# Half-and-half head layout for the first seven attention tiles, a key ring, and a new place for one gating product

## The chip, the cores and the metric

One Trainium2 chip, one of its cores. The metric is the device time of one execution in microseconds (us), taken over several runs; a trace of one profiled execution stands beside them. The engines are TensorE (PE in the rows; PEld is its weight load), VectorE (DVE), ScalarE (ACT), GpSimd (POOL) and SyncE (SP), which issues the transfers. A "q" behind an engine's name (DVEq) marks what its sequencer does.

## The reference

Local attention with a few global keys and a distance bias, followed by a channel mix with a sigmoid gate, all in float32. Cut to what matters:

```python
# q, k, v: (4, 8, 768, 64); n_global = 8; n_local = 96
scores = q @ k.T / 8 + bias(distance, head)      # kept where key < n_global or 0 <= rel < n_local
a = softmax(where(keep, scores, -1e9))
x = (a @ v) as (4, 768, 512)
xk, xr = mu * x + (1 - mu) * x_prev              # x_prev: one position earlier
out = sigmoid(xr @ w_r) * (relu(xk @ w_k) ** 2 @ w_v)
```

w_k is 512x1024, w_v 1024x512, w_r 512x512.

## The kernel before

The 3072 query rows are 24 tiles of 128 rows, six to a batch entry; t is a tile's place in its entry. The channel mix works on 12 chunks of two tiles each.

Attention, per tile (functions `load_tile`, `split_tile`, `scores`, `transposes`, `weighted`): queries and keys come with the 64 head dimensions on partitions. A tile's scores use 256 key columns, the 128 of the tile before (whose first 32 are replaced by the entry's first 32 keys from t = 2 on, because the global keys lie there) and its own 128; at t = 0 there are only its own. Scores of two heads go into one PSUM tile `s`. VectorE adds the pattern and reduces (line 294), ScalarE takes exponentials (295), VectorE makes the reciprocal of the sums (301, 302), GpSimd scales (305), TensorE transposes (316), ScalarE copies the result out (317), and TensorE multiplies with the values (333).

The first seven tiles (`NATIVE = 7`, tiles 0 to 6) use plain float32 matmuls (line 286); all later ones use two float32r products of a high and a low part (288, 289). The first seven have their heads on the lower 64 partitions; the upper 64 of two query buffers `qz` and two key buffers `kz` are set to zero once by GpSimd (lines 204 and 205). Line 222 loads a tile's queries, 225 its keys; 227 loads the whole tile before at t = 1; 229 and 230 load the first 32 keys and the other 96 of the tile before from t = 2 on. All go to the buffer `n % 2`.

The weights come as 64-bit words and are turned into float32 by ScalarE or GpSimd and VectorE (159 to 172, `weight_begin`); `weight_split` then makes a high part (179) and a low part on VectorE (180). There are 20 pieces: eight of w_k, four of w_r, eight of w_v. Chunk 0 uses the words themselves (lines 385, 406 and 439), and the splits are given out one at a time beside it; the later chunks use high and low parts (376 to 378).

`channel_mix` makes four tiles kp (two blocks of 128 features each), two tiles z for the gate and two tiles vps; the gating product `sig = vps * sigmoid(z)` (446) is on VectorE, and 447 writes the result. kp, z and vps share three PSUM buffers in turn, so the second kp tile of chunk 1 needs the buffer of chunk 0's first vps tile, and the third one that of the second.

At the end stands a branch: if the sizes were outside what the patterns cover, a general version (`wide`) would run; with these inputs it is skipped. Seven small VectorE instructions (lines 621 to 627) make the flag from the sizes, every engine reads it (629), and line 630 branches.

The order of instructions on each engine is not the order of the text: when the kernel is built, a scheduler plays the program through a cost model and puts each engine's instructions into a queue, which the engine then works off in order. `tc.issue_after(ins)` adds edges to it: what the block holds is queued behind `ins` on that instruction's engine, without a semaphore.

Of the kernel before, what the change touches and what calls it, by code (L numbers as in the profile page):

```python
# [9 lines left out]
F32 = mybir.dt.float32  # L10
# [5 lines left out]
ALU = mybir.AluOpType  # L16
# [3 lines left out]
B, H, S, D = 4, 8, 768, 64  # L20
DM, DF = 512, 1024
NT = S // 128
NTILES = B * NT
NCHUNK = NTILES // 2
NATIVE = 7
GMAX = 32
LMAX = 97
# [5 lines left out]
def tile_biased_attention_channel_mix(ctx: ExitStack, tc: tile.TileContext, qT, kT, v, n_sizes, mu_kr, w_k, w_v, w_r, q_rows, k_rows, v_rows, slopes, out):  # L33
    nc = tc.nc
    vec, act, pool, pe = nc.vector, nc.scalar, nc.gpsimd, nc.tensor
# [8 lines left out]
    ngf, nlf = sizes[:, 0:1], sizes[:, 1:2]  # L44
# [22 lines left out]
    p4k = fast.enter_context(tc.tile_pool(name="p4k", bufs=3))  # L67
    kw_pool = fast.enter_context(tc.tile_pool(name="kw", bufs=2))
# [105 lines left out]
    def weight_split(i):  # L174

        name, src, k, c = w_steps[i]
        word, hi = w_word.pop((name, k, c)), w_hi[name][:, k, c : c + 512]
        lo = w_low[name, k, c] = w_pool.tile([128, 512], F32R, tag="wl", name=f"w{name}_lo_{i}")
        (act.copy if i % 4 < 2 else pool_copy)(hi, word)
        vec.tensor_sub(lo, word, hi)  # L180

    w_count = [0, 0]

    def weights_go(begun):
        while w_count[0] < min(begun, len(w_steps)):
            weight_begin(w_count[0])
            w_count[0] += 1

    def splits_go(n):
        while w_count[1] < n:  # L190
            weight_split(w_count[1])
            w_count[1] += 1

    def pool_copy(dst, src):
        pool.tensor_scalar(dst, src, 1.0, 1.0, op0=ALU.mult, op1=ALU.mult)


    state = {}

    padded = []  # L200
    for i in range(2):
        qz = q_pool.tile([128, H, 128], F32, name=f"qz_{i}", tag="qh")
        kz = kw_pool.tile([128, H, 256], F32, name=f"kz_{i}", tag="kw")
        pool.memset(qz[64:128], 0.0)
        pool.memset(kz[64:128], 0.0)
        padded.append((qz, kz))

    def load_tile(n):
        b, t = divmod(n, NT)
        s = state[n] = {}  # L210
        native = n < NATIVE
        halves = (0,) if native else (0, 64)
        if native:
            qr, kr = padded[n % 2]
        else:
            qr = p4k.tile([128, H, 128], F32, tag="t4k", name=f"qraw_{n}")
            if n == NATIVE:
                kr = kw_pool.tile([128, H, 256], F32, tag="kw", name=f"kraw_{n}")
            else:
                kr = p4k.tile([128, H, 128], F32, tag="t4k", name=f"kraw_{n}")  # L220
        for o in halves:
            nc.sync.dma_start(qr[o : o + 64], qT[n])
        for o in halves:
            if n <= NATIVE:
                nc.sync.dma_start(kr[o : o + 64, :, 128:256], kT[n])
                if t == 1:
                    nc.sync.dma_start(kr[o : o + 64, :, 0:128], kT[n - 1])
                elif t:
                    nc.sync.dma_start(kr[o : o + 64, :, 0:32], kT[n - t, :, :, 0:32])
                    nc.sync.dma_start(kr[o : o + 64, :, 32:128], kT[n - 1, :, :, 32:128])  # L230
            else:
                nc.sync.dma_start(kr[o : o + 64], kT[n])
        s["qr"], s["kr"] = qr, kr
# [13 lines left out]
    def split_tile(n):  # L247
        t = n % NT
        s = state[n]
        s["sum"] = s_pool.tile([128, H], F32, name=f"sum_{n}", tag="sum")  # L250
        s["nmax"] = s_pool.tile([128, H], F32, name=f"nmax_{n}", tag="nmax")
        s["e"] = {}
        if n < NATIVE:
            return
        qh = q_pool.tile([128, H, 128], F32R, name=f"qh_{n}", tag="qh")
        ql = q_pool.tile([128, H, 128], F32R, name=f"ql_{n}", tag="ql")
        kw = kw_pool.tile([128, H, 256], F32R, name=f"kw_{n}", tag="kw")
        cur = kw[:, :, 0 if n == NATIVE and t else 128 : 256]
        kr = s["kr"]
        if n == NATIVE:  # L260
            kr = kr[:, :, 256 - cur.shape[2] : 256]
        pool_copy(qh, s["qr"])
        pool_copy(cur, kr)
        vec.tensor_sub(ql, s["qr"], qh)
        vec.tensor_sub(cur[64:128], kr[64:128], cur[64:128])
        if t and n > NATIVE:
            pk = state[n - 1]["kw"]
            if t == 1:
                pool_copy(kw[:, :, 0:128], pk[:, :, 128:256])
            else:  # L270
                pool_copy(kw[:, :, 32:128], pk[:, :, 160:256])
                pool_copy(kw[:, :, 0:32], pk[:, :, 0:32])
        s["qh"], s["ql"], s["kw"] = qh, ql, kw

    def scores(n, hp):
        t = n % NT
        s = state[n]
        c0 = 0 if t else 128
        w = 256 - c0
        p = pat if t else pat0  # L280
        ps = ps_s.tile([128, 512], F32, name=f"s_{n}_{hp}", tag="s")
        for u in range(2):
            h = 2 * hp + u
            o = ps[:, u * 256 : u * 256 + w]
            if n < NATIVE:
                pe.matmul(o, s["qr"][:, h, :], s["kr"][:, h, c0:256], start=True, stop=True)
            else:
                pe.matmul(o, s["qh"][:, h, :], s["kw"][:, h, c0:256], start=True, stop=False)  # L288
                pe.matmul(o, s["ql"][:, h, :], s["kw"][:, h, c0:256], start=False, stop=True)  # L289
        for u in range(2):  # L290
            h = 2 * hp + u
            o = ps[:, u * 256 : u * 256 + w]
            e = e_pool.tile([128, 256], F32, name=f"e_{n}_{h}", tag="e")
            vec.tensor_tensor_reduce(out=e[:, :w], in0=o, in1=p[:, h, :], op0=ALU.add, op1=ALU.min, scale=-0.125, scalar=3.0e38, accum_out=s["nmax"][:, h : h + 1])  # L294
            act.activation(e[:, :w], e[:, :w], AF.Exp, bias=s["nmax"][:, h : h + 1], scale=-1.0, accum_out=s["sum"][:, h : h + 1])  # L295
            s["e"][h] = e
        if hp % 2 == 0:
            return
        h0, nh = 2 * hp - 2, 4
        r = s_pool.tile([128, nh], F32, name=f"r_{n}_{hp}", tag="r", bufs=8)  # L300
        vec.tensor_scalar(r, s["sum"][:, h0 : h0 + nh], 1.0e-9, None, op0=ALU.add)
        vec.reciprocal(r, r)  # L302
        for u in range(nh):
            e = s["e"][h0 + u]
            pool.tensor_scalar(e[:, :w], e[:, :w], r[:, u : u + 1], 1.0, op0=ALU.mult, op1=ALU.mult)  # L305
# [62 lines left out]
    def channel_mix(xk, xr, out_rows, f_pool, f2_pool, ps_f, first=False):  # L368
# [6 lines left out]
        def three(o, sh, sl, mh, ml, first, last):  # L375
            pe.matmul(o, sh, mh, start=first, stop=False)  # L376
            pe.matmul(o, sh, ml, start=False, stop=False)  # L377
            pe.matmul(o, sl, mh, start=False, stop=last)  # L378
# [14 lines left out]
        for fp in range(4):  # L393
# [5 lines left out]
            for u in range(2):  # L399
                f = slice((2 * fp + u) * 128, (2 * fp + u + 1) * 128)  # L400
                c = fp // 2 * 512
                g = slice(f.start - c, f.stop - c)
                o = ps[:, u * 256 : (u + 1) * 256]
# [28 lines left out]
        for i in range(2):  # L432
            c = slice(i * 128, (i + 1) * 128)
            vp = ps_f.tile([128, 512], F32, name="vps", tag="f")
            sig = sigs[i][1]
            for f in range(8):
                if first:
                    weights_go(13 + f)
                    pe.matmul(vp, kk_all[:, f, c], w_word["v", f, 0], start=f == 0, stop=f == 7)
                    if i:  # L440
                        splits_ok[0] = 13 + f
                else:
                    splits_go(13 + f)
                    three(vp, kkh[:, f, c], kkl[:, f, c], w_hi["v"][:, f, :], w_low["v", f, 0], f == 0, f == 7)
                yield
            vec.tensor_mul(sig, vp, sig)  # L446
            nc.sync.dma_start(out_rows(i), sig)

    splits_ok = [0]

    def ffn(c):
        xt = state["x", c]
# [25 lines left out]
    for step in range(NTILES + 1):  # L478
# [4 lines left out]
        for hp in range(4):  # L483
# [18 lines left out]
            n = min(8, 2 + slot * 4 // 3) if slot < 6 else 8 + (slot - 5) * 6 // 7  # L502
# [115 lines left out]

    okf = const.tile([128, 2], F32, name="okf")
    wide_i = const.tile([1, 1], I32, name="wide_i")  # L620
    vec.tensor_scalar(okf[:, 0:1], nlf, float(LMAX), None, op0=ALU.is_le)
    vec.tensor_scalar(okf[:, 1:2], nlf, 1.0, None, op0=ALU.is_ge)
    vec.tensor_mul(okf[:, 0:1], okf[:, 0:1], okf[:, 1:2])
    vec.tensor_scalar(okf[:, 1:2], ngf, float(GMAX), None, op0=ALU.is_le)
    vec.tensor_mul(okf[:, 0:1], okf[:, 0:1], okf[:, 1:2])
    vec.tensor_scalar(okf[:, 0:1], okf[:, 0:1], -1.0, 1.0, op0=ALU.mult, op1=ALU.add)
    vec.tensor_copy(wide_i, okf[0:1, 0:1])

    need_wide = nc.values_load(wide_i[0:1, 0:1], min_val=0, max_val=1)
    with tc.If(need_wide > 0):  # L630
# [45 lines left out]
```

## Time and profile before

| | before |
|---|---|
| time, median of 3 runs | 522.92 us (522.72 to 523.63) |
| the profiled execution | 522.1 us |
| its span, first to last instruction | 520.3 us |
| mean granted TensorE clock | 0.988 |
| TensorE busy | 499.3 us (96%) |
| VectorE busy | 359.4 us (69%) |
| HBM read, written | 41.16 MB, 6.29 MB |

The span is what the trace shows; the time has 1.8 us more around it. Busy times are those of one execution. TensorE's matmuls overlap, and their ends are modelled, so that a busy TensorE is not one at its peak. A granted clock of 1.00 is 2.4 GHz, 0.50 is 1.2 GHz.

### The profile page before, as it was taken

To read this page: it belongs to the slowest core of one execution; us is meant where nothing else is said; L and a number is where in the kernel's file an instruction comes from. 1 tells how busy PE (TensorE), PEld (TensorE's weight loads), DVE (VectorE), ACT (ScalarE), POOL (GpSimd) and SP (SyncE) were. 2 spreads that over 40 slices of the span, in tenths; PEclk is the share of its full clock that TensorE was granted. 3 is DMA by queue.
4 is the path that set the end of the run, shared out by engine and by line. 5 is a ranking of instruction groups with operands and counts; after the bars stand their busy time and mean duration, and the time that the engine had idled before them with its cause. 6 is when DMAs were issued, how large, how long until landed. Compare 5 with 4: busy or idle time off the path is not lost.

```text
span 520.3 us, 9815 instructions
## 1 busy us (share of the span) xinstructions
PE 499.3 (96%) x3420; PEld 427.1 (82%) x3420; DVE 359.4 (69%) x856; ACT 311.1 (60%) x712; POOL 253.7 (49%) x392
## 2 busy tenths in 40 slices
PE   7978999889999999999999999999999999999995
PEld 5656864488898898898898898898898898898984
DVE  6869989877878858757768858757768855435321
ACT  4869653244658567567668567567668568544220
POOL 7657847318658536427538536427538535203000
PEclk9979999989999999999999999999999999999999
DMA  8997952411432422422322522423322210100101
GB/s 196 326 247 174 233 197 66 122 41 42 111 93 66 127 63 67 108 81 83 103 62 66 126 64 67 109 80 82 101 62 67 71 38 25 42 7 2 40 2 45
DMA packets 27304, 48.16 MB, mean 93 GB/s; under 512 B 7216, under 2 KB 13360, under 8 KB 27248
## 3 DMA queue, kind: packets, MB, share of 16 engines
q1 hardware_dynamic: 27104, 47.46, 34.3%
q8 instruction: 29, 0.48, 0.4%
q14 instruction: 27, 0.22, 0.1%
q10 hardware_dynamic: 144, 0.00, 0.0%
HBM read 41.16 MB, written 6.29 MB: 91 GB/s over the span
## 4 chain that ended last, share of the span: by engine, by line
PE 79%; DVE 2%; DMA 1%; issue 0%; POOL 0%; SPq 0%; DVEq 0%; POOLq 0%
PE kp L376 8%; PE vps L377 8%; PE vps L376 8%; PE kp L377 8%; PE kp L378 8%; PE vps L378 8%; PE av L333 7%; PE t L316 6%; PE z L376 4%; PE z L377 4%; PE z L378 4%; PE s L289 3%; PE s L288 3%; DMA qraw<-in_qT_dram 1%; DVE wv_lo L180 1%
## 5 line engine op out<-in xcount | busy, mean ns | idle before, releaser
L305 POOL TENSOR_SCALAR e<-e,r 128x256 f32<-128x256 f32 (+1 forms) x192 | 104.2, 562 | 151.1 <-DVE r L302 88.4
L295 ACT ACTIVATE e<-e,nmax 128x256 f32<-128x256 f32 (+1 forms) x192 | 92.9, 485 | 27.9 <-DVE nmax L294 23.9
L376 PE MATMUL kp<-xk_hi,wk_hi 128*128 128x256 f32 x352 | 100.2, 285 | 4.2 <-DVE sig L446 4.2
L378 PE MATMUL kp<-xk_hi,wk_lo 128*128 128x256 f32 x352 | 99.5, 283 | 0.0
L377 PE MATMUL kp<-xk_lo,wk_hi 128*128 128x256 f32 x352 | 99.4, 282 | 0.0
L294 DVE CUSTOM_DVE_ANT_0 e<-s,pat 128x256 f32<-128x256 f32 (+1 forms) x192 | 69.1, 395 | 34.4 <-PE s L289 22.0
L376 PEld LDWEIGHTS kp<-xk_hi,wk_hi 128*128 128x128 f32 x352 | 67.0, 190 | 5.1 <-DVE sig L446 4.4
L377 PE MATMUL vps<-wv_lo,kk_hi 128*128 128x512 f32 x176 | 69.9, 397 | 0.0
L376 PE MATMUL vps<-wv_hi,kk_hi 128*128 128x512 f32 x176 | 69.9, 397 | 0.0
L378 PE MATMUL vps<-wv_hi,kk_lo 128*128 128x512 f32 x176 | 69.2, 393 | 0.0
L377 PEld LDWEIGHTS kp<-xk_lo,wk_hi 128*128 128x128 f32 x352 | 66.7, 190 | 0.4
L378 PEld LDWEIGHTS kp<-xk_hi,wk_lo 128*128 128x128 f32 x352 | 66.7, 190 | 0.0
L317 ACT COPY et<-t 128x512 f32<-128x512 f32 (+1 forms) x96 | 52.1, 545 | 17.1 <-PE t L316 16.6
L316 PE MATMUL t<-ident,e 128*128 128x128 f32 x352 | 57.2, 281 | 4.6 <-POOL e L305 4.2
L419 DVE TENSOR_TENSOR kk<-kp,kk 128x512 f32<-128x512 f32 x44 | 30.4, 690 | 43.9 <-ACT kk L413 43.7
L316 PEld LDWEIGHTS t<-ident,e 128*128 128x128 f32 x352 | 42.2, 142 | 17.8 <-POOL e L305 7.0
L333 PE MATMUL av<-et,va 128*64 128x128 f32 x704 | 46.6, 278 | 1.5 <-ACT et L317 1.5
L333 PEld LDWEIGHTS av<-et,va 128*64 128x64 f32 x704 | 39.0, 136 | 10.3 <-issue 5.7
L421 DVE TENSOR_TENSOR kk_lo<-kk,kk_hi 128x512 fp32r<-128x512 f32 x44 | 32.6, 742 | 17.3 <-ACT kk_hi L420 17.1
L413 ACT ACTIVATE kk<-kp 128x512 f32<-128x512 f32 x48 | 28.3, 590 | 23.8 <-PE kp L378 23.0
L420 ACT CAST kk_hi<-kk 128x512 fp32r<-128x512 f32 x44 | 27.3, 621 | 24.9 <-DVE kk L419 24.9
L288 PE MATMUL s<-kw,qh 128*128 128x256 f32 (+1 forms) x136 | 40.4, 320 | 0.0
(109 smaller groups left out, 1030.0 us busy)
## 6 DMA issues: line engine op xcount, KB each, us to landing
kraw<-in_kT_dram SPq DMA_DIRECT2D x36, 256.0 KB, 4.1
qraw<-in_qT_dram SPq DMA_DIRECT2D x34, 256.0 KB, 4.3
va<-in_v_dram SPq DMA_DIRECT2D x24, 256.0 KB, 3.1
out_dram<-sig SPq DMA_DIRECT2D x24, 256.0 KB, 3.5
w<-in_w_k_dram SPq DMA_DIRECT2D x8, 512.0 KB, 8.2
w<-in_w_v_dram SPq DMA_DIRECT2D x8, 512.0 KB, 3.6
kz<-in_kT_dram SPq DMA_DIRECT2D x8, 256.0 KB, 6.2
w<-in_w_r_dram SPq DMA_DIRECT2D x4, 512.0 KB, 8.7
```

The lines of the kernel that those rows point to most:

```text
L288: pe.matmul(o, s["qh"][:, h, :], s["kw"][:, h, c0:256], start=True, stop=False)
L294: vec.tensor_tensor_reduce(out=e[:, :w], in0=o, in1=p[:, h, :], op0=ALU.add, op1=ALU.min, scale=-0.125, scalar=3.0e38, accum_out=s["nmax"] ...
L295: act.activation(e[:, :w], e[:, :w], AF.Exp, bias=s["nmax"][:, h : h + 1], scale=-1.0, accum_out=s["sum"][:, h : h + 1])
L305: pool.tensor_scalar(e[:, :w], e[:, :w], r[:, u : u + 1], 1.0, op0=ALU.mult, op1=ALU.mult)
L316: pe.transpose(pt[:, c : c + 128], e[:, k * 128 : (k + 1) * 128], ident)
L317: act.copy(et[:, : 2 * nb * 128], pt[:, : 2 * nb * 128])
L333: pe.matmul(o, vt[:, h * 64 : (h + 1) * 64], et[:, c : c + 128], start=k == 0, stop=k == nb - 1)
L376: pe.matmul(o, sh, mh, start=first, stop=False)
L377: pe.matmul(o, sh, ml, start=False, stop=False)
L378: pe.matmul(o, sl, mh, start=False, stop=last)
L419: vec.tensor_mul(kk, pv, kk)
L421: vec.tensor_sub(kkl[:, 2 * fp : 2 * fp + 2, :], kk, kkh[:, 2 * fp : 2 * fp + 2, :])
```

## The change

1. For the first seven tiles, heads 0 to 3 lie on the lower and heads 4 to 7 on the upper 64 partitions, of queries and keys alike. Only the queries have zeros: in the half that a head does not use. Queries and keys come in one transfer per half, four per tile. Keys go to a ring of four slots, and the keys of the tile before are read from its slot, so that a score tile takes two matmuls of 128 columns per head instead of one of 256. The first 32 keys of the entry are kept in `firsts` by a VectorE copy at t = 0, and another copy puts them over the first columns of a slot before it is used as "the tile before" of a tile with t >= 2.
2. The low parts of weights whose split is issued behind chunk 0's first gating product are queued behind it on VectorE.
3. The seven instructions of the size test are queued behind the last gating product.

```diff
@@ weight_split
         (act.copy if i % 4 < 2 else pool_copy)(hi, word)
-        vec.tensor_sub(lo, word, hi)
+        if last[0] is None:
+            vec.tensor_sub(lo, word, hi)
+        else:
+            with tc.issue_after(last[0]):
+                vec.tensor_sub(lo, word, hi)
@@
+    HH = H // 2
+    sides = ((0, 0), (64, HH))
     padded = []
     for i in range(2):
         qz = q_pool.tile([128, H, 128], F32, name=f"qz_{i}", tag="qh")
-        kz = kw_pool.tile([128, H, 256], F32, name=f"kz_{i}", tag="kw")
-        pool.memset(qz[64:128], 0.0)
-        pool.memset(kz[64:128], 0.0)
-        padded.append((qz, kz))
+        pool.memset(qz[64:128, 0:HH], 0.0)
+        pool.memset(qz[0:64, HH:H], 0.0)
+        padded.append(qz)
+    ring = kw_pool.tile([128, 4, HH, 128], F32, name="ring", tag="kw")
+    firsts = kw_pool.tile([128, HH, 32], F32, name="firsts", tag="kw")
@@ load_tile
+        if n < NATIVE:
+            qr, kr = padded[n % 2], ring[:, n % 4]
+            for o, h in sides:
+                nc.sync.dma_start(qr[o : o + 64, h : h + HH], qT[n, :, h : h + HH])
+                nc.sync.dma_start(kr[o : o + 64], kT[n, :, h : h + HH])
+            s["qr"], s["kr"] = qr, kr
+            return
@@ split_tile
         if n < NATIVE:
+            if t == 0:
+                vec.tensor_copy(firsts, s["kr"][:, :, 0:32])
             return
@@ scores
             if n < NATIVE:
-                pe.matmul(o, s["qr"][:, h, :], s["kr"][:, h, c0:256], start=True, stop=True)
+                if t:
+                    pe.matmul(o[:, 0:128], s["qr"][:, h, :], state[n - 1]["kr"][:, h % HH, :], start=True, stop=True)
+                pe.matmul(o[:, w - 128 : w], s["qr"][:, h, :], s["kr"][:, h % HH, :], start=True, stop=True)
@@
+        if hp == 3 and n + 1 < NATIVE and (n + 1) % NT >= 2:
+            vec.tensor_copy(s["kr"][:, :, 0:32], firsts)
@@ channel_mix
-            vec.tensor_mul(sig, vp, sig)
+            last[0] = vec.tensor_mul(sig, vp, sig).ins
             nc.sync.dma_start(out_rows(i), sig)
 
     splits_ok = [0]
+    last = [None]
@@ (the seven instructions of the size test)
+    with tc.issue_after(last[0]):
-    vec.tensor_scalar(okf[:, 0:1], nlf, float(LMAX), None, op0=ALU.is_le)
...
-    vec.tensor_copy(wide_i, okf[0:1, 0:1])
+        vec.tensor_scalar(okf[:, 0:1], nlf, float(LMAX), None, op0=ALU.is_le)
...
+        vec.tensor_copy(wide_i, okf[0:1, 0:1])
```

Tile 7, the first of the later kind, still loads its own keys and those of tile 6 to both halves.

## Rows read from the trace of the kernel before

**Rows 1.** The page: busy time, share and instructions of each engine.

```profile
PE 499.3 (96%) x3420; PEld 427.1 (82%) x3420; DVE 359.4 (69%) x856; ACT 311.1 (60%) x712; POOL 253.7 (49%) x392
```

**Rows 2.** The chain of waits in order of time: start us, us, what.

```profile
106.01 0.58 PE kp L376
```

**Rows 3.** Stretches: us, busy of each engine (instructions), granted clock, DMA share, GB/s.

```profile
28.00:30.00 2.00, 0.71 (x10) 0.42 (x8) 2.00 (x5) 2.00 (x6) 1.88 (x3) 1.00 1.33 173
...
30.00:40.00 10.00, 8.75 (x34) 6.90 (x35) 5.80 (x23) 5.25 (x16) 5.38 (x9) 0.66 1.11 293
...
106.00:108.00 2.00, 1.99 (x9) 1.99 (x10) 1.97 (x4) 0.00 (x0) 0.00 (x0) 0.50 0.36 135
```

**Rows 4.** Timeline of the start: start us, us, engine, line, operation, [idle before].

```profile
5.56 1.94 POOL L205 MEMSET kz<- 64x2048 f32 x1
5.69 1.89 DVE L128 TENSOR_SCALAR btmp<-btmp,sizes 128x96 f32<-128x96 f32 x1
...
8.11 0.22 DVE L129 COPY btmp<-btmp 128x128 f32<-128x128 f32 x1
...
9.61 0.28 DVE L294 CUSTOM_DVE_ANT_0 e<-s,pat 128x128 f32<-128x128 f32 x1
...
10.04 0.14 DVE L626 TENSOR_SCALAR okf<-okf 128x1 f32<-128x1 f32 x1
```

**Rows 5.** Timeline of TensorE from 20 to 33 us.

```profile
20.01 1.97 PE L286 MATMUL s<-kz,qz 128*128 128x256 f32 x8 [0.20 <-DMA kz<-in_kT_dram]
...
31.94 0.69 PE L316 MATMUL t<-ident,e 128*128 128x128 f32 x2 [0.71 <-POOL e L305]
32.60 3.75 PE L286 MATMUL s<-kz,qz 128*128 128x256 f32 x8
```

**Rows 6.** Single lines: L230 from 12 to 24 us, L222 from 130 to 131.

```profile
L230 SPq DMA_DIRECT2D kz<-in_kT_dram x2: 628/948/1267, 13.4 to 22.2; - x2
...
DMA to landing us min/median/max: 6.4/8.4/10.3
...
L222 SPq DMA_DIRECT2D qraw<-in_qT_dram x2: 471/530/588, 130.2 to 130.7; - x2
...
DMA to landing us min/median/max: 3.6/3.9/4.1
```

**Rows 7.** Timelines of VectorE and TensorE from 101 to 111 us.

```profile
101.49 0.68 DVE L180 TENSOR_TENSOR wr_lo<-word,wr_hi 128x512 fp32r<-128x512 f32 x1
102.28 3.08 DVE L180 TENSOR_TENSOR wv_lo<-word,wv_hi 128x512 fp32r<-128x512 f32 x4
105.27 0.68 DVE L446 TENSOR_TENSOR sig<-vps,sig 128x512 f32<-128x512 f32 x1
...
106.47 0.68 DVE L446 TENSOR_TENSOR sig<-vps,sig 128x512 f32<-128x512 f32 x1
...
106.01 0.58 PE L376 MATMUL kp<-xk_hi,wk_hi 128*128 128x256 f32 x1 [4.17 <-DVE sig L446]
...
106.61 0.42 PE L378 MATMUL kp<-xk_hi,wk_lo 128*128 128x256 f32 x1
106.82 0.41 PE L376 MATMUL kp<-xk_hi,wk_hi 128*128 128x256 f32 x1
...
110.72 0.28 PE L376 MATMUL kp<-xk_hi,wk_hi 128*128 128x256 f32 x1
```

**Rows 8.** The end: timeline, then lines L629 and L630 (ns min/median/max, start).

```profile
514.82 0.69 DVE L446 TENSOR_TENSOR sig<-vps,sig 128x512 f32<-128x512 f32 x1 [4.93 <-PE vps L378]
...
L629 DVEq TENSOR_LOAD <-wide_i x1: 547/547/547, 514.9 to 514.9; - x1
...
L630 PEldq COMPARE_BRANCH  x1: 3742/3742/3742, 511.1 to 511.1; - x1
...
L630 DVEq COMPARE_BRANCH  x1: 72/72/72, 515.5 to 515.5; - x1
...
L630 DVEq EVENT_SEMAPHORE  x1: 21/21/21, 518.6 to 518.6; - x1
```

More of the change, by code (lines that the diff above doesn't have):

```diff
@@ L210, in load_tile @@
         s = state[n] = {}
[L211 to L214, printed above, removed]
-        else:
-            qr = p4k.tile([128, H, 128], F32, tag="t4k", name=f"qraw_{n}")
+        if n < NATIVE:
[5 more added lines that the diff above has]
+            return
+        qr = p4k.tile([128, H, 128], F32, tag="t4k", name=f"qraw_{n}")
+        if n == NATIVE:
+            kr = kw_pool.tile([128, H, 256], F32, tag="kw", name=f"kraw_{n}")
+        else:
+            kr = p4k.tile([128, H, 128], F32, tag="t4k", name=f"kraw_{n}")
+        for o in (0, 64):
+            nc.sync.dma_start(qr[o : o + 64], qT[n])
+        for o in (0, 64):
             if n == NATIVE:
[L218 to L224, printed above, removed]
                 nc.sync.dma_start(kr[o : o + 64, :, 128:256], kT[n])
@@ L620, in tile_biased_attention_channel_mix @@
     wide_i = const.tile([1, 1], I32, name="wide_i")
-    vec.tensor_scalar(okf[:, 0:1], nlf, float(LMAX), None, op0=ALU.is_le)
[L622 to L626, printed above, removed]
-    vec.tensor_copy(wide_i, okf[0:1, 0:1])
+    with tc.issue_after(last[0]):
+        vec.tensor_scalar(okf[:, 0:1], nlf, float(LMAX), None, op0=ALU.is_le)
+        vec.tensor_scalar(okf[:, 1:2], nlf, 1.0, None, op0=ALU.is_ge)
+        vec.tensor_mul(okf[:, 0:1], okf[:, 0:1], okf[:, 1:2])
+        vec.tensor_scalar(okf[:, 1:2], ngf, float(GMAX), None, op0=ALU.is_le)
+        vec.tensor_mul(okf[:, 0:1], okf[:, 0:1], okf[:, 1:2])
+        vec.tensor_scalar(okf[:, 0:1], okf[:, 0:1], -1.0, 1.0, op0=ALU.mult, op1=ALU.add)
+        vec.tensor_copy(wide_i, okf[0:1, 0:1])
     need_wide = nc.values_load(wide_i[0:1, 0:1], min_val=0, max_val=1)
```

## Prediction

> **What bounds the kernel now.** I read the profiled execution in this order: the page's busy shares, the chain of waits, the busy time by stretches, and then the timeline and single lines of the stretches that stood out. TensorE is busy for 96% of the span [rows 1], and from 106.01 us on the chain of waits is almost all TensorE [rows 2]: behind that point the time is TensorE's own work, and the change takes none of it away. So the change is worth what it moves that point forward, plus or minus what it does to the few microseconds behind the last matmul. Ahead of 106 us TensorE is not the limit, and three places are to be seen there. At the start GpSimd's memsets hold VectorE up [rows 4]. Between 28 and 40 us the DMA engines are fully taken and yet move only 173 GB/s, VectorE is idle for 4.2 of 10 us and the granted clock averages 0.66 [rows 3]. At 106.01 TensorE has stood still for 4.17 us, waiting for the first gating product (line 446) [rows 7].
>
> The profiled execution took 522.1 us, of which 520.3 are its span; the median of the three timed runs is 522.92, or 0.8 more. I make the sum against 522.1 and add 0.8.
>
> **The start.** Of the memsets, the two of 64x2048 (keys) go and the two of 64x1024 (queries) become four of 64x512. The last one now takes 1.94 us for 2048 columns and ends at 7.50; a quarter of it, 0.5 us, is my estimate for 512. VectorE's instruction at 5.69 lasts 1.89 us for 96 columns and ends at 7.58, just as that memset does; a copy of 128 columns behind it takes 0.22 [rows 4]. Four more behind it end with it, and all stand ahead of the first score reduction at 9.61. Without the long memset I put that at 8.0: 1.6 us earlier. The seven instructions of the size test, 0.14 us each [rows 4], leave this stretch too. The six added copies of first keys (at the tiles of t = 0, and ahead of tiles 2 to 5) are of 128x128: 0.22 us each by the copy above, 1.3 us in all. Four of them stand where VectorE waits for the same score matmuls anyway, and it is idle for 4.2 us between 30 and 40 us [rows 3]; I cost them at nothing, and at 1.3 us without that cover.
>
> **Tile loads and the ring.** A tile of t >= 2 now loads 512 KB of q and k in four transfers of 128 KB, where it loaded 768 KB. In all, 1.31 MB of earlier keys (five tiles, 256 KB each) are not loaded again: at 173 GB/s [rows 3] 7.6 us of the DMA engines. The other 3.67 MB go half to each partition half. Two later loads of 256 KB to the two halves, issued at 130.2 and 130.7, land 3.6 and 4.1 us after that, so 1.05 us apart or 250 GB/s [rows 6]. That makes 14.7 us in place of 21.2; 14.1 us are saved in all. What does it end? Tile 3's last key transfer, issued at 22.2, lands 10.3 us later at 32.5 [rows 6], and its first score matmul starts at 32.60; tile 2's at 20.01 also follows a key load [rows 5]. But the transpose at 31.94 had waited 0.71 us for GpSimd, and it stands ahead of tile 3 in TensorE's queue [rows 5]. With its load early, tile 3 gains the 1.6 us of the start and some 0.5 of its own, 2.1. Its first eight score matmuls took 3.75 us at the low clock (1.2 GHz), against 1.97 for tile 2 at 2.4 GHz [rows 5]; if the idle time in front of them shrinks enough for the clock to stay up, that and the transposes beside them bring 2.5 more, and scores ordered ahead of the waiting transposes up to 1.5. The bounds are 0 (other waits take over) and 6.1. I take 4.0, in the upper half, since the memsets and both tiles' loads move together and VectorE has idle time to follow.
>
> The Trainium skill (SBUF — State Buffer, Can I just issue two DMAs to hit both halves?) holds that transfers to the two halves serialize, which the pair above bears out; the same page (Door 1: The DMA port swizzle) has 196 GB/s for 64 partitions, where the pair shows 250. By 196 the saving would be 10.1 us, and in that proportion (an estimate) 2.9 in place of the 4.0 and a sum of 518.0.
>
> TensorE issues 160 score matmuls of 128 columns in place of 80 of 256: the same columns, and weights load beside matmuls. In this stage it is not the limit; I cost that at nothing. The ring lets keys be issued early (a slot is written again four tiles later), while queries still have two buffers. SP issues four transfers per tile instead of two to four.
>
> **The first gating product.** On VectorE today: the last low part of w_r until 102.17, four low parts of w_v (3.08 us), the product at 105.27, one low part, the second product at 106.47 [rows 7]. TensorE's second kp tile has waited for the first product since 101.84. If that stands ahead of the four, it starts at 102.28 and TensorE goes on 0.74 us later (as from 105.27 to 106.01): at 103.0, 3.0 us earlier. Behind the long stop the granted clock is 0.50 [rows 3] and kp matmuls start 0.21 us apart [rows 7], so 0.11 at full clock; some 13 of them run so, and I count their 1.3 us as won, because the stop shrinks to 1.2. VectorE's work up to the second product is the same, so TensorE can't use that product's buffer before 107.2. It would be ready at 103.0 + 28 x 0.11 = 106.1 (18 kp matmuls, four scores, six kp) and waits 1.1. Sum: 3.0 + 1.3 - 1.1 = 3.2 us. Bounds: 4.3, and 0.9, if all eight low parts (0.77 each) land between the products; the second then lets TensorE go at 109.8, where its next kp tile now starts at 110.7 [rows 7].
>
> **The end.** The size test now sits behind the last product on VectorE. Before, its last steps were done at 10 us [rows 4], and each engine read the flag beside its last work. Now the product ends at 515.51, seven dependent instructions of 0.15 us make 1.05, then every engine reads the flag (0.55 us on VectorE) and branches, and VectorE's next instruction comes 3.1 us behind its branch [rows 8]: 520.3 in place of 518.6, or 1.7 later. SP's closing run of semaphores waits for the output transfer anyway, and some 0.5 us of it will be done before. I take +1.2, with bounds 0.7 and 2.5 (TensorE's branch shows 3.74 us [rows 8], but it stood behind matmuls).
>
> **Sum.** 522.1 - 4.0 - 3.2 + 1.2 = 516.1; with 0.8 for the median, 516.9 us. Its own range is 513.2 (522.9 - 6.1 - 4.3 + 0.7) to 520.1 (522.9 - 2.1 - 3.2 + 2.5).
>
> **The rivals.**
> A, more: the freed DMA time lets the whole first stage close up, 8.5 us instead of 4. 522.9 - 8.5 - 3.2 + 1.2 = 512.4. For it: the DMA engines are fully taken; against it: VectorE would have no idle time left.
> B, the transfers were hidden anyway: the transposes that wait for GpSimd set tile 3, and 1.0 us of the start is left. 522.9 - 1.0 - 3.2 + 1.2 = 519.9. For it: the wait at 31.94.
> C, the reordering does not do what it says: an edge can push low parts behind the product without bringing the product forward, or put all eight between the products. 522.9 - 4.0 - 0.9 + 1.2 = 519.2.
> D, B and C together: 522.9 - 1.0 - 0.9 + 1.2 = 522.2.
> E, slower: VectorE works its queue in order, and the first-key copies at tiles 0 and 6 wait for a key transfer. If the scheduler puts them ahead of ready work, reductions and weight words wait behind them, and TensorE behind those. Two key transfers landed 6.4 and 10.3 us after their issue [rows 6]; two waits of 4.5 us would make 516.9 + 9 = 525.9. It decides from 6.0 us of such waits on. Against it: at tile 0 the first matmul waits for the same load.
> F, each transfer pays its landing in series: of the 3.6 us of the pair above, 1.05 is moving, and 2.5 would be paid per transfer. Four per tile would bring tiles 2 and 3 some 4 us later each: 522.9 + 8 - 3.2 + 1.2 = 528.9. The pair's landings, 1.05 us apart, speak against it. The Trainium skill (SBUF — State Buffer, The DMA setup-cost knee) has a fixed cost of about 2 us per transfer.
>
> **How the numbers follow.** Forecast 0.53, A 0.10, B 0.11, C 0.09, D 0.06, E 0.08, F 0.03. About 0.2% (1.05 us) is what a measurement of this kernel can tell from no change. Faster: forecast, A, B and C make 0.83, less 0.02 for the weak ends of B and C, 0.81. Same: D and those 0.02, 0.08. Slower: E and F, 0.11. The range goes from 511.5 (0.03 of A below it) to 522.4 (E, F and 0.02 of D above it) and leaves out 0.16.
>
> **What would show it.** Right: a first reduction near 8 us; tile 3's scores before 30 us; a granted clock near 1.00 between 30 and 40 us; TensorE's stop at the first product near 1 us with no low clock behind it; some 6 us from the last product to the end in place of 4.8. Wrong: the transposes ahead of tile 3 still waiting for GpSimd past 31 us (B), a stop of 3 us or more behind the first kp tile (C), VectorE idle on a copy that waits for a key load (E), key loads that land over 2 us apart (F), or a tail of 8 us.

## Result and profile after

The changed kernel takes 517.81 us (median of four runs, 517.28 to 518.97) against 523.27 for the kernel before, measured beside it: a ratio of 0.990, with a 95% interval of 0.9879 to 0.992. The forecast of 516.9 was 0.9 too low, inside its range. Its terms did not come out as the sum has them, though, and most of what follows is about that. The profiled execution is the slowest of the four, 518.97 us with a span of 517.2, and that of before (522.1) is shorter than all four runs of before that its time stands for (522.72 to 523.63). So the two traces differ by 3.1 us where the medians differ by 5.5, and 2.3 us of the gain are in no trace.

The page of the changed kernel, busy times, and DMA packets of before and then of after:

```profile
PE 498.5 (96%) x3500; PEld 429.7 (83%) x3500; DVE 359.2 (69%) x862; ACT 310.8 (60%) x712; POOL 252.8 (49%) x392
...
DMA packets 27304, 48.16 MB, mean 93 GB/s; under 512 B 7216, under 2 KB 13360, under 8 KB 27248
...
DMA packets 20538, 46.88 MB, mean 91 GB/s; under 512 B 3200, under 2 KB 5248, under 8 KB 20480
```

Beside [rows 1], TensorE has 80 matmuls more (each plain float32 one is recorded as two) and nearly the same busy time. 1.28 MB and 6,766 packets are gone.

Stretches, with the columns of [rows 3]: first 8 to 12 us of before, then four stretches of after.

```profile
8.00:12.00 4.00, 2.75 (x13) 2.40 (x11) 3.23 (x25) 3.22 (x13) 2.29 (x6) 1.00 1.12 272
...
8.00:12.00 4.00, 3.94 (x27) 3.69 (x26) 2.57 (x21) 3.43 (x17) 1.55 (x5) 1.00 0.67 176
...
20.00:30.00 10.00, 9.14 (x59) 7.77 (x60) 7.20 (x23) 5.70 (x17) 6.40 (x10) 0.66 1.04 310
30.00:40.00 10.00, 8.94 (x78) 7.46 (x77) 9.62 (x35) 8.95 (x27) 8.02 (x11) 1.00 1.06 259
106.00:108.00 2.00, 2.00 (x20) 2.00 (x19) 1.32 (x3) 1.11 (x2) 0.00 (x0) 1.00 0.00 0
```

The low clock between 30 and 40 us is gone, but the stretch before it now has the 0.66 [rows 3]: it was moved, not removed. From 8 to 12 us the DMA engines, full before, are busy for 0.67 only. At 106 us TensorE runs at full clock.

The start of after, timeline (columns as in [rows 4]), then SP's transfers of w_k's first four pieces (L159) and tile 2's two key transfers (L222):

```profile
3.66 0.52 POOL L210 MEMSET qz<- 64x512 f32 x1
...
6.24 0.72 POOL L125 TENSOR_SCALAR pat<-btmp 128x128 bf16<-128x128 f32 x2 [1.85 <-DVE btmp L119]
...
7.04 1.72 POOL L137 TENSOR_SCALAR pat<-btmp 128x256 bf16<-128x256 f32 x4
7.44 0.21 DVE L264 COPY firsts<-ring 128x128 f32<-128x128 f32 x1
7.57 0.28 DVE L309 CUSTOM_DVE_ANT_0 e<-s,pat 128x128 f32<-128x128 f32 x1
...
L159 SPq DMA_DIRECT2D w<-in_w_k_dram x4: 333/431/437, 8.8 to 10.1; - x4
...
L222 SPq DMA_DIRECT2D ring<-in_kT_dram x2: 597/676/754, 11.5 to 12.9; - x2
...
DMA to landing us min/median/max: 8.1/8.3/8.5
```

The last long memset takes 0.52 us (0.5 was put) and ends at 4.18; the first score reduction starts at 7.57 instead of 9.61. Then SP stands: the transfer of w_k's piece 0 needs the buffer in which the pattern was built (`btmp`), and GpSimd's last pattern step ends at 7.04 + 1.72 = 8.76. It issues at 8.79; four pieces of 512 KB stand ahead of tile 2's loads, whose keys, issued at 11.5 and 12.9, land only by 12.9 + 8.5 = 21.4. TensorE meets that, and its clock falls; tile 3's first score matmul is the last line:

```profile
19.24 0.68 PE L298 MATMUL s<-ring,qz 128*128 128x128 f32 x4 [1.18 <-DMA qz<-in_qT_dram]
...
21.55 0.77 PE L299 MATMUL s<-ring,qz 128*128 128x128 f32 x2 [0.70 <-DMA ring<-in_kT_dram]
...
30.87 0.49 PE L298 MATMUL s<-ring,qz 128*128 128x128 f32 x2
```

TensorE and VectorE around the first gating product of after (before: [rows 7]):

```profile
95.29 0.28 PE L393 MATMUL kp<-xk_hi,wk_lo 128*128 128x256 f32 x1
95.50 2.02 PE L348 MATMUL av<-et,va 128*64 128x128 f32 x32
97.45 0.66 PE L331 MATMUL t<-ident,e 128*128 128x128 f32 x4
97.94 0.61 PE L299 MATMUL s<-ring,qz 128*128 128x128 f32 x4
98.31 0.36 PE L391 MATMUL kp<-xk_hi,wk_hi 128*128 128x256 f32 x1
...
96.16 0.68 DVE L461 TENSOR_TENSOR sig<-vps,sig 128x512 f32<-128x512 f32 x1
96.76 0.68 DVE L184 TENSOR_TENSOR wv_lo<-word,wv_hi 128x512 fp32r<-128x512 f32 x1
...
100.45 0.69 DVE L461 TENSOR_TENSOR sig<-vps,sig 128x512 f32<-128x512 f32 x1
```

The 4.17 us stop [rows 7] has gone altogether. The product stands ahead of w_v's low parts; but TensorE's queue is another one too. Halfway through the first kp tile stand 40 matmuls of attention (95.50 to 98.31), and by the time the second kp tile comes the product is long done.

The end of after, timeline and then reads of the flag (L646) and branches (L647), as in [rows 8]:

```profile
509.11 0.69 DVE L461 TENSOR_TENSOR sig<-vps,sig 128x512 f32<-128x512 f32 x1 [4.93 <-PE vps L393]
509.72 0.14 DVE L638 TENSOR_SCALAR okf<-sizes 128x1 f32<-128x1 f32 x1
...
510.72 0.14 DVE L644 CAST wide_i<-okf 1x1 int32<-1x1 f32 x1
...
L646 DVEq TENSOR_LOAD <-wide_i x1: 542/542/542, 510.9 to 510.9; - x1
...
L647 DVEq COMPARE_BRANCH  x1: 72/72/72, 511.5 to 511.5; - x1
...
L647 DVEq EVENT_SEMAPHORE  x1: 21/21/21, 515.4 to 515.4; - x1
```

The product ends at 509.80, the span at 517.2: a tail of 7.4 us, where it was 520.3 - 515.5 = 4.8.

For the account I summed, over TensorE's matmuls, the time from one start to the next beyond what the matmul takes at full clock (idle and slow time, us). That step is read from steady stretches, so an entry is good to some 0.3 us; a stretch covers the same time, not the same work, in each kernel:

| stretch | 0-10 | 10-20 | 20-30 | 30-40 | 40-60 | 60-100 | 100-110 | 110-140 |
|---|---|---|---|---|---|---|---|---|
| before | 3.95 | 3.67 | 3.39 | 4.02 | 4.37 | 2.91 | 5.79 | 0.09 |
| after | 2.92 | 4.30 | 4.19 | 2.52 | 4.06 | 2.34 | 0.09 | 1.74 |
| test behind first product | 2.48 | 4.79 | 3.59 | 2.89 | 3.54 | 2.13 | 0.06 | 1.40 |
| that, and two pieces ahead of tile 2 | 2.47 | 1.53 | 2.90 | 2.72 | 5.70 | 1.17 | 0.03 | 0.41 |

By the traces of before and after: -2.0 up to 100 us, -5.7 at the stop, +1.65 in new waits up to 140, +0.6 for the matmuls themselves (80 more of them), +2.6 at the end. That makes -2.9; the spans differ by 3.1. (The last two rows are experiments, below; the trace of the last one is of its shortest run.)

### The profile page after: what moved, and what is told of

It is laid out like the page before. It is cut to its first block, busy times and chain, and to the rows that moved or that the text cites. A ratio compares the mean times of both kernels' runs of the same rounds, so it can differ in the third digit from the quotient of the medians.

```text
span 517.2 us, 9995 instructions
## 1 busy us (share of the span) xinstructions
PE 498.5 (96%) x3500; PEld 429.7 (83%) x3500; DVE 359.2 (69%) x862; ACT 310.8 (60%) x712; POOL 252.8 (49%) x392
## 4 chain that ended last, share of the span: by engine, by line
PE 76%; DVE 9%; DMA 6%; POOL 3%; issue 2%; ACT 2%; SPq 0%; POOLq 0%; ACTq 0%; DVEq 0%
PE vps L392 7%; PE vps L391 7%; PE kp L391 7%; PE kp L392 7%; PE kp L393 7%; PE vps L393 7%; PE t L331 7%; PE av L348 7%; PE z L391 4%; PE z L392 4%; PE z L393 4%; PE s L302 3%; DMA ring<-in_kT_dram 3%; PE s L301 3%; DMA w<-in_w_v_dram 3%
## 5 line engine op out<-in xcount | busy, mean ns | idle before, releaser
L320 POOL TENSOR_SCALAR e<-e,r 128x256 f32<-128x256 f32 (+1 forms) x192 | 105.8, 568 | 144.6 <-DVE r L317 97.2
L332 ACT COPY et<-t 128x512 f32<-128x512 f32 (+1 forms) x96 | 52.3, 545 | 14.5 <-PE t L331 14.1
L393 PEld LDWEIGHTS vps<-wv_hi,kk_lo 128*128 128x128 f32 x176 | 33.1, 188 | 8.2
```

Of the source, the lines that this page charges most:

```text
L332: act.copy(et[:, : 2 * nb * 128], pt[:, : 2 * nb * 128])
```

## Experiments

Eleven kernels ran, each beside the kernel before (522.5 to 522.6 us, measured anew with each of three groups). The changed kernel was not run again beside them: its 517.81 stands beside 523.27, so that a difference to it is uncertain by some 0.7 us more, and the ratios are the safer comparison.

| kernel | us (lowest to highest) | ratio to before, 95% |
|---|---|---|
| e1_product_only | 518.56 (517.95-520.82) | 0.991-0.9938 |
| e2_layout_only | 517.89 (517.14-519.01) | 0.9904-0.9934 |
| e3_test_at_end | 525.09 (523.84-527.49) | 1.0039-1.0082 |
| e4_test_early | 517.63 (516.72-518.32) | 0.989-0.9921 |
| e5_pieces_reordered | 519.90 (516.99-520.75) | 0.9917-0.9956 |
| e6_product_held_back | 519.38 (518.19-520.01) | 0.9924-0.9954 |
| e7_old_memsets | 519.38 (518.08-522.55) | 0.9927-0.9961 |
| e9_old_key_traffic | 524.76 (522.88-528.13) | 1.0028-1.0066 |
| e10_test_mid | 515.77 (515.14-516.64) | 0.9856-0.9894 |
| e11_tile2_third | 512.85 (510.60-514.32) | 0.9794-0.9838 |
| e12_tile2_first | 518.60 (515.50-520.37) | 0.9896-0.9952 |

**The three parts alone.** First the product's edge on the kernel before:

```diff
-        vec.tensor_sub(lo, word, hi)
+        if last[0] is None:
+            vec.tensor_sub(lo, word, hi)
+        else:
+            with tc.issue_after(last[0]):
+                vec.tensor_sub(lo, word, hi)
...
+            last[0] = vec.tensor_mul(sig, vp, sig).ins
```

> The kernel before with only the new place of the first gating product (the low parts behind it queued behind it); old layout, size test where it was. Theory (the stop at 106 us and its low clock are worth 3 to 6 us and the later waits give part of it back): 3.2 to 4.5 us faster than before, 518.8 to 520.1. Rival (the product is not brought forward by the edge alone, the whole gain is the layout's): within 1 us of before, 522 to 524.

Measured: 4.0 us less, as the theory has it. VectorE does the product right behind w_r's last low part, and TensorE waits 0.74 us for it, with the granted clock at 1.00 behind (this trace is of the longest of its six runs, 520.82):

```profile
103.59 0.69 DVE L181 TENSOR_TENSOR wr_lo<-word,wr_hi 128x512 fp32r<-128x512 f32 x1
104.20 0.69 DVE L450 TENSOR_TENSOR sig<-vps,sig 128x512 f32<-128x512 f32 x1
104.80 0.69 DVE L184 TENSOR_TENSOR wv_lo<-word,wv_hi 128x512 fp32r<-128x512 f32 x1
...
104.94 0.39 PE L380 MATMUL kp<-xk_hi,wk_hi 128*128 128x256 f32 x1 [0.74 <-DVE sig L450]
```

Then the layout alone: the changed kernel without both kinds of edges (`weight_split` and the size test as before).

> The changed kernel without both kinds of edges: the new layout, ring and copies alone. Theory (the first stage gave 2 us by the count of TensorE's idle time, and the stop in front of the second kp tile comes back): 1.5 to 3 us faster than before, 520.3 to 521.8, with a stop of 3 us or more behind the first kp tile. Rival (the layout alone removes the stop, since everything ahead of it is earlier): 5 us or more faster, 518 or less, and no such stop.

Measured: 4.6 less; the theory falls, the rival holds (by its time of 518 or less; it had put the gain at 5 or more). Without any edge VectorE puts two low parts of w_v ahead of the product (97.59), and there is no stop at all. The two parts are not additive: -4.0 and -4.6 alone, and -4.9 together with the test as before (e4, below). The forecast had added them.

The size test's edge, on the kernel before (the `with tc.issue_after(last[0])` around its seven instructions):

> The kernel before with only the size test queued behind the last gating product. Theory (the engines read the flag and branch only after the last product): 1.2 to 2.6 us slower than before, 524.4 to 525.9, all of it behind the last product; from the last product's end to the end of the span 6 to 7.4 us in place of 4.8. Rival (the test in the first 10 us cost VectorE as much as it costs at the end): within 0.5 us of before.

Measured: 2.6 more, the upper end. Not all of it is shown to lie behind the last product: in the trace the tail is 7.0 us instead of 4.8, which makes 2.2. And taken out of the changed kernel again:

> The changed kernel with the size test free again, the rest as changed. Theory (its new place costs what the last product's tail grew, 1.2 to 2.6 us): 515.2 to 516.6 us, the span's part behind the last product back at 4.8 us. Rival (early test instructions delay the first stage by as much): 517 to 518.5.

Measured: 517.63, the rival's range, although the tail is back at 4.9. The two kernels' queues differ in the seven instructions alone, so the 2.6 were lost again somewhere earlier. GpSimd's pattern steps and SP's transfers of w_k's pieces in this run (compare L125, L137 and L159 of the changed kernel, above):

```profile
6.44 1.47 POOL L125 TENSOR_SCALAR pat<-btmp 128x128 bf16<-128x128 f32 x2 [2.04 <-DVE btmp L119]
7.98 1.73 POOL L137 TENSOR_SCALAR pat<-btmp 128x256 bf16<-128x256 f32 x4
...
L159 SPq DMA_DIRECT2D w<-in_w_k_dram x3: 334/430/431, 9.7 to 10.6; - x3
```

Three of the seven stand among the steps that build the pattern. GpSimd begins 0.20 us later, and its first step takes 1.47 instead of 0.72 (VectorE's six pattern steps beside it, L123, take 0.90 instead of 1.32, so one is faster where the other is slower; why was not separated); it ends at 9.71 instead of 8.76. SP gets past piece 0 at 9.74 instead of 8.79, and the first plain kp matmul comes at 50.0 instead of 47.9. The test's old place was not free: all that stands behind piece 0 in SP's queue was later for it.

**The stop on the new layout.** The product emitted behind four low parts of w_v, with an edge to the fourth; the low parts without edges:

```diff
+                if first and i and f == 4:
+                    held(low_ins[15])
...
+            if first and i == 0:
+
+                def held(ins, vp=vp, sig=sig):
+                    with tc.issue_after(ins):
+                        vec.tensor_mul(sig, vp, sig)
```

> The changed kernel with its layout and its size test at the end, but the first gating product queued behind four low parts of w_v on VectorE, as it stood before; the low parts have no edge. It prices the layout without the end of the stop. Theory (the first stage is worth about 2 us by the two traces, and the rest of the layout's gain is the stop): TensorE stands 3 us or more at that product again with a low clock behind it, and the time is 521.5 to 523.5, that is 522.5 - 2.0 + 2.6. Rival (the first stage is worth the 4.0 of the prediction): 519.5 to 521.2, that is 522.5 - 4.0 + 2.6 and some of it lower.

Measured: 519.38, 0.1 below the rival's range; the theory falls. The product starts at 99.21, 3.05 us later than in the changed kernel, and yet:

```profile
99.95 0.39 PE L387 MATMUL kp<-xk_hi,wk_hi 128*128 128x256 f32 x1 [0.34 <-DVE sig L463]
```

0.34 us of waiting, no low clock behind it. What removes the stop in the changed kernel is the attention work that its order puts inside the first kp tile. What the edge adds there stays open: e2 and e4, without and with it, are 0.3 apart, but e6 is 1.6 us above the changed kernel and the intervals of the ratios do not meet; its trace shows only the 0.34 at the product, and the rest was not found. In e11, below, four score matmuls alone stand inside that tile. The product, at 94.97 right behind w_r's last low part, lets TensorE go at 95.71 (0.74 later), and the second kp tile starts at 95.94: there the edge may count, which was not tried.

**What the first stage waits for.** The old traffic put back (tiles 1 to 5 load the earlier keys again, into a part of a buffer that nothing reads):

```diff
+                if t:
+                    again = big[o : o + 64, 512 * (1 + t % 3) : 512 * (2 + t % 3)]
+                    nc.sync.dma_start(again.rearrange("p (h k) -> p h k", h=HH), kT[n - 1, :, h : h + HH])
```

> The changed kernel with the earlier keys loaded again for tiles 1 to 5, two transfers of 128 KB per tile into a buffer that nothing reads: the 1.31 MB that the change saved, at the new rate of two halves. Theory (the DMA engines are what the first stage waits for): each tile's transfers end 1 us later, tiles 2 to 5 add up to 2 to 4 us, and the time is 519.8 to 522.0. Rival (the transfers are hidden behind VectorE and GpSimd): 517.0 to 518.8.

Measured: 7 us more than the changed kernel, beyond the theory's own range. The transfers were not hidden: with the old traffic the layout and the product's edge together make up for the 2.6 us of the test and little more. But the ten transfers also take SP 0.47 to 0.61 us each and stand in its queue ahead of later loads, so how much is their bytes and how much their place was not separated. Two stretches of it:

```profile
20.00:30.00 10.00, 8.47 (x48) 7.02 (x47) 6.51 (x19) 3.97 (x10) 5.85 (x8) 0.66 0.94 256
...
40.00:50.00 10.00, 8.09 (x50) 6.64 (x50) 10.00 (x27) 9.62 (x29) 8.01 (x10) 0.66 0.73 189
```

A second stretch at the low clock comes in, from 40 to 50 us (another, 0.57 from 8 to 12 us, is in the trace of e2 as well); the extra transfers' own time (ten of about 0.5 us, an estimate by 250 GB/s) would make 5 of the 7.

The old memsets put back (two of 64x1920, over a part of that buffer):

> The changed kernel with two more memsets of 64x1920 on GpSimd at the start (as much as the two of 64x2048 that the change removed), over a part of the first-keys buffer that nothing reads. Theory (tile 2's transfers come too late for the start to count): the first score reduction goes from 7.6 back to 9 or later, but the first kp matmul stays within 0.8 us of 47.9 and the time is 517.0 to 518.6. Rival (as the prediction put it, the 1.6 us of the start pass through the whole stage): 519.0 to 520.0.

Measured: 519.38, the rival's range, but it doesn't tell the two apart: the first reduction moved by 0.85 us only (8.42), and the new instructions also changed SP's order (one piece at 6.9, the others from 9.6). What the start alone is worth stays open. In its trace tile 2's keys land at 19.4, 2 us before the changed kernel's, and the clock is 1.00 from 10 to 30 us (0.89 from 40 to 50), yet it is no faster: when tile 2 lands does not decide the time by itself.

SP's stand at piece 0 taken away:

```diff
+    w_steps[0:4] = w_steps[1:4] + w_steps[0:1]
```

> The changed kernel, but the four pieces of w_k for the first columns are begun in the order 1, 2, 3, 0. In the changed kernel piece 0 comes first, its buffer is the one that the pattern's scratch tile uses, and SP stands before its transfer from 6.84 to 8.79 us; the four pieces then move ahead of tile 2's queries and keys, which land at 19.1 to 21.4. Theory (the transfers set the first stage, and the gain was halved by this order in SP's queue): tile 2's keys land by 16, the low clock from 19.9 goes or moves, the first plain kp matmul comes 1.5 to 3 us before 47.9, and the time is 514.8 to 516.5. Rival (what stands behind the transfers, VectorE and GpSimd, sets the stage): tile 2's keys land early, but the first kp matmul stays within 0.8 us and the time is 517.0 to 518.5.

Measured: 519.90, 2.1 above the changed kernel, though the intervals of the ratios just meet. Both fall: the pieces are issued from 6.9 on, tile 2's loads 1.4 us earlier, and they land later, by 22.35:

```profile
L160 SPq DMA_DIRECT2D w<-in_w_k_dram x4: 328/430/430, 6.9 to 8.8; - x4
...
DMA to landing us min/median/max: 3.7/8.9/11.8
...
21.24 1.19 PE L299 MATMUL s<-ring,qz 128*128 128x128 f32 x4 [4.33 <-DMA qz<-in_qT_dram]
```

TensorE stands 4.33 us for tile 2's queries. With four pieces ahead of tile 2, an SP that no longer waits does not bring it in earlier. (Why the second of them landed 4.65 us behind the first, where 1.3 is usual, the trace doesn't show.)

**Order of the queue, and a better version.** First the size test behind the first gating product instead of the last:

```diff
+            gates.append(last[0])
...
-    with tc.issue_after(last[0]):
+    with tc.issue_after(gates[0]):
```

> The changed kernel, but the seven instructions of the size test are queued behind the first gating product instead of the last one. Theory: in the run with the test early, its seven instructions stood ahead of the pattern's last steps, so that SP got past the transfer of w_k's piece 0 at 9.74 us instead of 8.79 and everything behind it was later; at the end the test costs 2.6. Behind the first product (96 us) it stands on neither path: the first kp matmul stays near 47.9, the tail is 4.7 to 5.0 and the time is 514.8 to 516.4. Rival (the early test costs nothing, and the first stage only scatters from run to run, or SP's read of the flag holds back transfers behind it): 517.0 to 518.5.

Measured: 515.77, as the theory has it, though its interval still meets the changed kernel's. It takes the early place of the changed kernel (SP passes piece 0 at 8.79) and the old tail of 4.85:

```profile
L649 DVEq COMPARE_BRANCH  x1: 72/72/72, 508.5 to 508.5; - x1
...
L649 DVEq EVENT_SEMAPHORE  x1: 21/21/21, 511.4 to 511.4; - x1
```

Then, on top, only two of w_k's pieces (1 and 2) ahead of tile 2's loads, the others behind:

```diff
+    w_steps[0:4] = w_steps[1:4] + w_steps[0:1]
...
-            n = min(8, 2 + slot * 4 // 3) if slot < 6 else 8 + (slot - 5) * 6 // 7
+            n = (2, 2, 2, 2, 4, 6)[slot] if slot < 6 else 8 + (slot - 5) * 6 // 7
```

> The kernel with the test behind the first product, and besides w_k's pieces begun in the order 1, 2, 3, 0 and only two of them ahead of tile 2's queries and keys, the others behind. Theory (between 12 and 40 us the DMA engines are full, so that the order of the queue decides, and no transfer gets faster): two pieces fill the idle DMA time from 9 to 12, tile 2's keys land by 17 instead of 21.4, the low clock from 19.9 goes or gets shorter, and the time is 513.0 to 515.3. Rival (the sum of the traffic sets the stage whatever its order): within 0.8 us of the kernel with the test behind the first product, 515.0 to 517.0.

Measured: 512.85, the best of all, 0.15 below the theory's range and 9.8 us below the kernel before; its interval lies apart from that of e10. The trace is of the shortest of its five runs, 510.60, where the longest is 514.32. Stretches, and tile 2's key transfers:

```profile
8.00:12.00 4.00, 3.63 (x30) 3.46 (x31) 2.96 (x23) 3.83 (x19) 2.15 (x6) 1.00 0.98 365
...
20.00:30.00 10.00, 9.04 (x81) 6.96 (x80) 9.26 (x28) 8.74 (x27) 9.67 (x13) 1.00 1.04 307
...
L223 SPq DMA_DIRECT2D ring<-in_kT_dram x2: 594/594/595, 8.4 to 9.8; - x2
...
DMA to landing us min/median/max: 4.8/5.0/5.1
```

The DMA engines are busy from 8 us on, tile 2's keys land by 9.8 + 4.8 = 14.6 instead of 21.4, and the clock stays at 1.00 from 20 to 30 us.

At last none of the pieces ahead of tile 2, with the test behind the first product, `w_steps` as in the changed kernel and `(0, 0, 0, 0, 4, 6)`:

> As the one before, but none of w_k's pieces stands ahead of tile 2's queries and keys, in the order 0, 1, 2, 3. Theory (order decides): tile 2's keys land by 14.5, but the DMA engines stay idle from 9 to 11, so that weights and later tiles come some 1 to 2 us later: better than four pieces ahead, not better than two, 513.5 to 516.0. Rival (only the amount counts, and idle DMA time is lost): 516.5 to 518.5.

Measured: 518.60, 0.1 above the rival's range. Tile 2's keys land earliest of all, at 12.7, but:

```profile
8.00:12.00 4.00, 3.58 (x30) 3.41 (x30) 2.96 (x23) 3.83 (x19) 2.19 (x6) 1.00 0.56 185
...
20.00:30.00 10.00, 7.78 (x65) 6.61 (x63) 8.62 (x26) 6.06 (x17) 3.67 (x5) 0.83 1.05 258
30.00:40.00 10.00, 7.43 (x42) 5.98 (x40) 7.96 (x27) 7.38 (x21) 8.53 (x15) 0.83 1.05 277
```

the DMA engines have little to do from 8 to 12 us (0.56), the weights and tile 3 come later than in e11 (tile 3's keys at 26.2 instead of 25.0, and TensorE waits 1.20 us for them), and the low clock comes twice. My reading is that both count: the DMA engines must not run dry while SP waits for tile 0's query buffer, and no more than that may stand ahead of tile 2. It is not shown in full. In e10 the share from 8 to 12 us is 0.63, hardly more, and tile 3's keys land at 28.1, later than in e12; only w_k's four pieces come earlier there, by 18.8 instead of 21.5, and TensorE's order is another one. e11 differs from both in the order of the pieces too.

## Why the prediction was right, and where it was not

**What bounds the kernel** held: behind the first products the time is TensorE's, and the change was worth what it moved ahead of them.

**The start** came as put, 7.57 against 8.0, and no copy of first keys made VectorE wait for a key load (rival E): the one at 7.44 takes 0.21 and the reduction follows it at once; the only one that waited, at 30.38, waited 0.51 us for score matmuls. But the 1.6 us did not carry on: tile 2's scores start at 19.24 instead of 20.01. The step followed VectorE alone and left out SP's queue: GpSimd's part of the pattern holds it until 8.79, and four pieces of w_k stand ahead of tile 2's loads. Which of the two matters how much is not settled: without the hold alone these come no earlier (e5).

**Tile loads and the ring**, 4.0: the traces give 2.0, half of it, though the saving of traffic was not hidden (e9, with the doubt named there; and no transpose ahead of tile 3 waits for GpSimd past 31 us, so not rival B). Of its signs, tile 3's scores before 30 us did not come: they start at 30.87 instead of 32.60, 1.7 earlier where 2.1 and more were put. Three of the term's parts failed. The 2.5 us for the clock were not won: TensorE's stand for tile 2's queries and keys (1.18 and 0.70 us) went with a low clock ten microseconds earlier. The 173 GB/s are those of 28 to 30 us alone, when 709 of 783 packets had under 512 B (earlier keys); from 30 to 40 us it was 293 [rows 3]. Tile 2's own queries and keys landed 1.29 and 1.48 us behind the transfer ahead, 203 and 177 GB/s, and from 12 to 40 us the DMA engines moved 294 GB/s before and 287 after: the layout saved bytes, but the rise of the rate from 173 to 250, 6.5 of the 14.1 us, does not show in the whole. And the sum had tile 3's load to move, while tile 2's landed later than before, 21.4 against 19.9 (issued at 13.4 and landed 6.4 later, [rows 6]): SP's queue had four pieces of w_k ahead of it, where three had been issued by 6 us before. The working never asked what the new order of SP's queue would be. e11 shows what lay there: with another order of the same transfers it is 2.9 us below e10. Even then, and in its shortest run, the table's stretches up to 100 us give 5.8 us against before, not the 8.5 of rival A. Fixed costs in series (F) did not show. By the Trainium skill (SBUF — State Buffer, The DMA setup-cost knee) a transfer has about 2 us that don't scale with its bytes. In a queue that is not empty this trace doesn't show them between landings: tile 2's four halves landed 0.45, 0.52, 1.08 and 0.71 us apart, 512 KB in 2.75 us or 191 GB/s, tile 3's in 1.97 us or 266 GB/s, around the 250 of the sum.

**The first gating product**, 3.2: alone it gave 4.0 (e1), inside the bounds. In the changed kernel the stop gave back all of its 5.7 us, less the 1.65 of new waits behind it, 4.05, so the size was 0.85 too small and the reason half wrong: the layout's own order does it without the edge (e2), and what the edge adds is not shown (e2 and e4 against e6). C's mechanism, an edge that does nothing, was thus perhaps there, without C's price. The step that failed is the assumption that TensorE's queue stays as it was while the parts are added.

**The end**, 1.2: 2.55 by the trace, above the upper bound of 2.5, and 2.2 (trace) to 2.6 (median) by e3. The seven instructions made 1.06 as put, and the read of the flag, which had overlapped with the product, 0.65. Mis-sized were two parts: VectorE's next instruction came 3.9 us behind its branch instead of 3.1, 0.85 more, and the 0.5 us of SP's closing semaphores were not saved, since these now wait for VectorE (the last of them comes 0.3 to 0.4 behind it, before and after). Nor did every engine read the flag beside its last work before: SP did so at 17.7 us.

**Copies, the added matmuls**: the copies cost nothing; the matmuls 0.6 us instead of nothing.

So the forecast came within 0.9 us of the median with errors of +2.0 (early), +1.4 (end), +0.6 (matmuls) and about -0.8 (stop less new waits). They add up to some 3 us, which is what the traces miss the forecast by; the median is nearer because the profiled execution of before lies 1.2 us below the median (523.27) and that of after 1.2 above its own. The signs of the terms were right. Their order was not: the tile loads, put first, gave the least of the three, and the stop the most. The sum was luckier than its parts.

## What to carry to other kernels

Where a transfer queue is full, ask of a change to the loads not only what it saves but what then stands ahead of what, and which wait at the head of the queue leaves the DMA engines dry: here two pieces ahead of a tile beat four and none. Two repairs of one stop need not add up (4.0 and 4.6 alone, 4.9 together); run each alone before their sum is written down. In this kernel a small test that every engine waits for did best neither ahead of the first work nor behind the last, but beside a stretch with slack (517.63 early, 517.81 at the end, 515.77 between).

## What the hardware showed unexpectedly

With the flag made at the end, four engines branch at 511.4 to 511.5 and SP at 511.8; VectorE goes on 3.9 us behind its branch, ScalarE and GpSimd 0.4. Where they branch one after the other (e10), it is 2.9 for VectorE, 0.5 for ScalarE and 3.9 for GpSimd. In the end-placed test on the old layout (e3) VectorE took 3.6. Whether the engines hold each other up there was not tried.

Weights, queries and keys share the DMA engines unevenly: with all of them busy from 12 to 40 us the changed kernel moved 287 GB/s on the mean, in short stretches between 164 and 418, and a 512 KB piece took between 1.25 and 2.8 us to land behind the one ahead of it.
